# A gated mixer and state-space kernel: first layer in three tiles of 128 channels and one of 64 with stacked parts, gate sums from refetched tokens, column means on TensorE

## Chip, cores and metric

The kernel runs on one core of one Trainium2 chip. The metric is the device time of one execution in microseconds. Before the change the median of three runs is 380.77 us, from 379.42 to 381.68.

## What is computed

`x` is 2048 tokens of D = 448 channels. A sigmoid gate per token blends a state-space convolution `a` of x with a small mixer `b`:

```python
h = gelu(layernorm(x) @ w1)                      # 448 -> 448, in four groups of 112 channels
hs = concat(group 0 shifted by +1 token, group 1 by -1, group 2 by +2, group 3 by -2) @ w2
x1 = x + hs
b = x1 + gelu(layernorm(x1) @ w3) @ w4           # 448 -> 1792 -> 448
a = long_convolution(x, K) + x * D_skip
g = sigmoid((x * gate_w).sum(-1))
out = g * a + (1 - g) * b
```

The convolution's kernel K comes from 256 complex states per channel (`log_A_real`, `A_imag`, `C_real`, `C_imag`, `log_dt`). The kernel computes it by a short expansion with moments of the states, and falls back to a general path only if a guard on the data says so, which is not the case here.

## The kernel before

Tokens go in four blocks of 512, each of four chunks of 128. The matmuls are in fp32 with both factors split into a hi and a lo part, and three products are added: hi by hi, lo by hi, hi by lo.

The work is a list of 72 units. Unit n of the first 16 is a group of the shift mixer, by block in the order of groups 0, 2, 1, 3; then 56 units follow, 14 tiles of 128 channels of the second layer's 1792 for each block. Each unit has the same form:
- `first(n)`: 11 matmuls of 512 columns into a PSUM tile `p` (four k-tiles hi by hi, three lo by hi, four hi by lo). Line 437.
- `act_head(n)`: for the mixer's units a multiplication by the reciprocal deviation of each token, `rb`, on VectorE (446) and a gelu on ScalarE (456); for the others a gelu straight from PSUM (459). `act_copy(n)` rounds the result to the hi part `uh` (468), `act_tail(n)` subtracts to get the lo part `ul` on VectorE (472).
- `second(n)`: 12 matmuls of 448 columns into four PSUM tiles `acc0` to `acc3` (499), one for each chunk of the block. The last two units are in `last_two` (520).

The units 0 to 3, the loads, the splitting of W1 and W2 and the statistics of the first tokens are written out by hand in `begin()`. From unit 4 on a loop runs one iteration per unit: `first(n + 2)`, the gelu and copy of unit n + 2, the subtraction of unit n + 1, and `second(n)`. What else has to be done is put into the iterations by a table: `at(n, fn, ..., when=)` with the places before, after, between and late of iteration n. Instructions are issued on every engine in the order in which this code writes them, so the table sets what stands in front of what on each engine's queue. From iteration `OWN` on, VectorE gets the pieces of the convolution from a queue by credit.

Loads go through `room()`, which gives out three staging buffers in turn (two of the tag `raw`, one `rawc`); a load waits on SyncE (SP) until the buffer's last reader is done, and the loads behind it in SP's queue wait with it. `ld3(c)` and `ld4(i)` load pieces of W3 and W4, `sp3` and `sp4` split them: the hi part on ScalarE and the lo part on VectorE (217, 218). `ssm_par(q)` loads half of the states' parameters, `pk` (565), `ssm_exp(q)` takes their exponential (568, after a table load) and, for q = 0, a precise exponential of `log_dt` into `dts` on VectorE (65 to 79, 572, 573); `ssm_scale_par(k)` scales on ScalarE (580), and `ssm_moment(k, m)` are the moments on VectorE (586 to 599). `norm_d`, `norm_turn`, `norm_fetch`, `norm_hi` and `norm_lo` normalize a block, turn it over DRAM and split it for the second layer (382 to 406). `stats_b`, `rstd` and `rstd_rows` give means, reciprocal deviations and their rows (286 to 337); `rstd_rows` is a set of transposes on TensorE (336) and a copy on ScalarE (337).

The gate's weighted sum comes from extra columns of W1 in groups 0 and 1: `logits` copies its row out of PSUM (540) to DRAM, `logits_in` brings it back, `gates` transposes it and takes the sigmoid (554, 555), and `weigh` (410) uses it. The sums over the rows of W1 that centre it are added on GpSimd (`pool_sum`, 729 to 731) and turned into means by one matmul a group (`col_means`, 734). `keep_warm(4)` issues four matmuls into a bank that nobody reads (720).

## Time and profile before

| | before |
| --- | --- |
| median of 3 runs | 380.77 us (379.42 to 381.68) |
| the profiled execution | 380.4 us, span 378.6 us |
| granted TensorE clock | 0.997 |
| TensorE busy | 368.5 us, 97% |
| VectorE busy | 295.8 us, 78% |
| ScalarE busy | 210.2 us, 56% |
| GpSimd busy | 71.1 us, 19% |
| chain that ended last | 90% on TensorE: first layer (line 437) 46%, second layer (line 499) 43% |

The span is the time from the first to the last instruction of the profiled execution; its own time includes 1.8 us around it. Busy times are of instructions that overlap in part on TensorE, so a busy TensorE is not one at its peak. The chain of waits follows the work back from the last instruction, at each step to what released it. PE is TensorE, PEld its weight loads, DVE VectorE, ACT ScalarE, POOL GpSimd, SP and SPq SyncE and its queue of transfers. In the text iteration n is the loop's n, and unit n is finished in it by `second(n)`.

### The profile page before, as it was taken

How to read it: one execution, taken by the hardware profiler on the slowest of the kernel's cores; microseconds unless marked ns; L12 is line 12 of the kernel's file. 1: busy time of each engine (PE TensorE's matmuls, PEld its weight loads, DVE VectorE, ACT ScalarE, POOL GpSimd, SP SyncE). 2: the span in 40 equal slices, each digit the busy share in tenths (PEclk: the TensorE clock that was granted, in tenths of full speed). 3: DMA queues.
4: the chain of work that ended last, by engine and by line, in shares of the span. 5: the costliest groups of instructions: out<-in, count | busy, mean ns of one | idle time of the engine just before them, and what ended most of it. 6: DMA issues, size and time to landing. Idle time of an engine off the chain costs nothing.

```text
span 378.6 us, 5180 instructions
## 1 busy us (share of the span) xinstructions
PE 368.5 (97%) x1713; PEld 314.6 (83%) x1713; DVE 295.8 (78%) x527; ACT 210.2 (56%) x349; POOL 71.1 (19%) x187
## 2 busy tenths in 40 slices
PE   7998999999999999999999999999999999999993
PEld 4786888888888888888888888888888888888883
DVE  4888979785858981998399989999787999996312
ACT  4764646546978467643465575465756654442220
POOL 3200070322000000040023536324041440000000
PEclk9999999999999999999999999999999999999998
DMA  8970606166615219000843515256685311372202
GB/s 266 397 265 1 224 1 173 30 118 209 209 56 157 46 50 214 3 0 12 243 72 78 83 29 153 63 160 124 97 183 134 78 28 19 73 189 48 77 0 102
DMA packets 85896, 42.26 MB, mean 112 GB/s; under 512 B 67030, under 2 KB 80614, under 8 KB 85226
## 3 DMA queue, kind: packets, MB, share of 16 engines
q1 hardware_dynamic: 85434, 41.20, 41.6%
q10 hardware_dynamic: 432, 0.70, 0.6%
q8 instruction: 15, 0.25, 0.3%
q14 instruction: 15, 0.12, 0.1%
HBM read 30.86 MB, written 11.02 MB: 111 GB/s over the span
## 4 chain that ended last, share of the span: by engine, by line
PE 90%; DVE 3%; ACT 2%; DMA 2%; issue 1%; POOL 0%; SPq 0%; DVEq 0%
PE p L437 46%; PE acc L499 43%; DMA w1r<-w_in 2%; PE acc L520 1%; ACT uh L468 1%; ACT uf L456 1%; PE misc L336 0%; DVE uf L446 0%; DVE z L638 0%; DVE w2l L218 0%; DVE b L286 0%; ACT w2h L217 0%; ACT xn L294 0%; DVE ul L472 0%; DVE xh L365 0%
## 5 line engine op out<-in xcount | busy, mean ns | idle before, releaser
L459 ACT ACTIVATE uf<-p 128x512 f32<-128x512 f32 x56 | 33.4, 597 | 101.9 <-PE p L437 101.8
L472 DVE TENSOR_TENSOR ul<-uf,uh 128x512 fp32r<-128x512 f32 (+1 forms) x72 | 48.9, 680 | 31.5 <-ACT uh L468 31.4
L638 DVE TENSOR_TENSOR_SCAN z<-z,carry 128x512 f32<-128x512 f32 x48 | 61.5, 1281 | 4.6 <-ACT z L633 0.7
L437 PE MATMUL p<-xh,w3h 128*128 128x512 f32 x224 | 61.3, 396 | 0.0
L437 PE MATMUL p<-xh,w3l 128*128 128x512 f32 x224 | 60.7, 392 | 0.0
L499 PE MATMUL acc<-w4h,uh 128*128 128x448 f32 x216 | 55.8, 364 | 0.3 <-DVE xs L508 0.3
L499 PE MATMUL acc<-w4h,ul 128*128 128x448 f32 x216 | 55.7, 364 | 0.0
L499 PE MATMUL acc<-w4l,uh 128*128 128x448 f32 x216 | 55.7, 363 | 0.0
L437 PEld LDWEIGHTS p<-xh,w3l 128*128 128x128 f32 x224 | 42.1, 188 | 9.9
L437 PE MATMUL p<-xl,w3h 128*128 128x512 f32 x168 | 48.0, 394 | 0.0
L437 PEld LDWEIGHTS p<-xh,w3h 128*128 128x128 f32 x224 | 42.0, 188 | 6.7
L468 ACT ACTIVATE uh<-uf 128x512 fp32r<-128x512 f32 (+1 forms) x72 | 45.6, 633 | 2.3
L499 PEld LDWEIGHTS acc<-w4h,uh 128*128 128x128 f32 x216 | 40.5, 188 | 6.6 <-issue 0.7
L499 PEld LDWEIGHTS acc<-w4l,uh 128*128 128x128 f32 x216 | 40.5, 188 | 3.1
L499 PEld LDWEIGHTS acc<-w4h,ul 128*128 128x128 f32 x216 | 40.5, 188 | 2.9
L633 ACT ACTIVATE z<-zs,nu 128x512 f32<-128x512 f32 x64 | 42.2, 710 | 0.8 <-DMA zs<-xT_in 0.4
L632 POOL COPY z<-carry 128x1 f32<-128x1 f32 x48 | 34.6, 731 | 17.4 <-DVE zs L644 17.1
L437 PEld LDWEIGHTS p<-xl,w3h 128*128 128x128 f32 x168 | 31.5, 188 | 7.2
L323 POOL TENSOR_TENSOR t<-r 128x4 f32<-128x4 f32 (+1 forms) x15 | 6.8, 453 | 133.2 <-DVE r L321 132.5
L640 POOL COPY carry<-z 128x1 f32<-128x1 f32 x48 | 14.1, 294 | 92.4 <-DVE z L638 91.5
L456 ACT ACTIVATE uf<-uf 112x512 f32<-112x512 f32 x16 | 10.1, 630 | 24.2 <-DVE uf L446 24.1
L638 DVE TENSOR_TENSOR_SCAN z<-z,carry,zero 128x512 f32<-128x512 f32 x16 | 20.0, 1247 | 0.0
(150 smaller groups left out, 496.5 us busy)
## 6 DMA issues: line engine op xcount, KB each, us to landing
zs<-xT_in SPq DMA_DIRECT2D x4, 1024.0 KB, 8.1
yd<-yt SPq DMA_DIRECT2D x56, 64.0 KB, 2.0
ysb<-yd SPq DMA_DIRECT2D x16, 224.0 KB, 3.0
out_dram<-xs SPq DMA_DIRECT2D x16, 224.0 KB, 2.8
raw<-xb_in SPq DMA_DIRECT2D x3, 1032.0 KB, 7.9
...
```

The costliest lines, as they stand in the source:

```text
L323: eng.tensor_mul(t, y, y)
L437: nc.tensor.matmul(p[:m, t0:t1], (wl if w else wh)[:, k, :], (xl if x_ else xh)[:, k, o + t0:o + t1], start=(q == 0 and fresh), stop=stop ...
L456: nc.scalar.activation(UF[n][:m], UF[n][:m], AF.Gelu_apprx_tanh)
L459: nc.scalar.activation(UF[n][:m], P1[n][:m], AF.Gelu_apprx_tanh)
L468: nc.scalar.activation(UH[n][:m], UF[n][:m], AF.Copy)
L472: nc.vector.tensor_sub(UL[n][:m], UF.pop(n)[:m], f32(UH[n][:m]))
L499: nc.tensor.matmul(ACC[j], (UL if p == 2 else UH)[n][:m, t], wl if p == 1 else wh, start=s and p == 0, stop=e and p == 2)
L520: nc.tensor.matmul(ACC[j], (UL if p == 2 else UH)[m][:, t], wl if p == 1 else wh, start=False, stop=m > n and p == 2)
L632: nc.gpsimd.tensor_copy(z4[:, m, 0:1], carry[:, k, m:m + 1])
L633: nc.scalar.activation(z4[:, m, 1:], ZS[b][:, k, :], AF.Copy, scale=nu[:, k, m:m + 1])
L638: nc.vector.tensor_tensor_scan(z, z, up, carry[:, k, m:m + 1], OP.add, OP.add)
L640: nc.gpsimd.tensor_copy(carry[:, k, m:m + 1], z[:, TB - 1:])
```

## The change

Group 2 of the first layer keeps 64 of its 112 channels in a tile of its own. Its weights lie side by side, 64 columns of hi parts and 64 of lo parts (`w1d`), so that one pass over the hi tokens gives both products, and `first` of that unit has 7 matmuls (4 with hi tokens, 3 with lo tokens). ScalarE copies the last 64 rows out of PSUM and VectorE adds the halves (`act_add`). After the gelu the hi part goes to the first 64 rows and the lo part to the last 64 rows of one tile, against rows of W2 that are repeated, so that `second` of that unit has 8 matmuls. The other 48 channels ride, 16 each, in the tiles of groups 0, 1 and 3, which have now 128 channels. They need another token shift than the group in whose tile they are: ScalarE takes the gelu of their 16 rows from shifted columns, and a few columns from the block before, kept in `skew`. For the first block those come from a small computation of the first two tokens (`first_tokens`, `first_skew`).

The tiles have no room left for the gate's columns, so `logits`, `logits_in` and the transposing matmul go. The tokens are fetched again (`gate_fetch`), multiplied and summed on VectorE (`gate_sum`) in the iterations 18 to 25, and `gates` makes the sigmoid from an exponential in iteration 27. `weigh` moves to iteration 28 and later.

The means of W1's rows are formed by TensorE alone (`col_means`, four matmuls a group), and `pool_sum` goes. `keep_warm` isn't called any more. In the table, the statistics of blocks 0 and 1, pieces of W3 and W4, the second parameters and the moments get other iterations.

The core of the diff:

```diff
-GW = G + 2
+GX = 128 - G
+GD = G - 3 * GX
+TI = {0: 0, 1: 1, 3: 2}
+W1O = {0: 0, 2: 512, 1: 768, 3: 1280}
...
-OWN = 34
+OWN = 35
...
-    w1h, w1l = wpair([128, 4, 4, GW], "w1")
-    w2h, w2l = wpair([G, 4, D], "w2")
-    w1r = big.tile([128, 4, 4, GW], F32, name="w1r", tag="w4al")
+    w1h, w1l = wpair([128, 3, 4, 128], "w1")
+    w1d = big.tile([128, 4, 128], F32R, name="w1d", tag="w4bh")
+    w2h, w2l = wpair([128, 4, D], "w2")
+    w1r = big.tile([128, 4 * D], F32, name="w1r", tag="w4al")
+    W1R = {g: w1r[:, o:o + 4 * (GD if g == 2 else 128)].rearrange("p (k m) -> p k m", k=4) for g, o in W1O.items()}
...
-            m = GW if i < 2 else G
-            wh, wl = w1h[:, i, :, :m], w1l[:, i, :, :m]
+            wh, wl = (w1d, None) if i == 2 else (w1h[:, TI[i]], w1l[:, TI[i]])
             o = HALO - SHIFT[i]
...
-        every = [(w, x_, k, 0, TB) for w, x_, r in ((0, 0, 4), (1, 0, 4), (0, 1, 3)) for k in range(r)]
+        every = [(w, x_, k, 0, TB) for w, x_, r in ((0, 0, 4), (1, 0, 4), (0, 1, 3)) for k in range(r)
+                 if not w or wl is not None]
         for q, (w, x_, k, t0, t1) in enumerate(seq or every):
-            nc.tensor.matmul(p[:m, t0:t1], (wl if w else wh)[:, k, :], (xl if x_ else xh)[:, k, o + t0:o + t1],
+            nc.tensor.matmul(p[:, t0:t1], (wl if w else wh)[:, k, :], (xl if x_ else xh)[:, k, o + t0:o + t1],
                              start=(q == 0 and fresh), stop=stop if q + 1 == len(seq or every) else False)
...
+    def act_add(n, part=None):
+        p = P1[n]
+        if not part:
+            UF[n] = wk.tile([128, TB], F32, name="uf")
+            nc.scalar.activation(UF[n][:GD], p[GD:], AF.Copy)
+        if part is not False:
+            nc.vector.tensor_add(UF[n][:GD], p[:GD], UF[n][:GD])
+
+    MUL, EDGE = set(), {}
+
+    def act_mul_first(rows):
+
+        MUL.add(0)
+        nc.gpsimd.memset(UF[0][:, 0:1], 0.0)
+        nc.vector.tensor_mul(UF[0][:, 1:], UF[0][:, 1:], rows[:, :TB - 1])
+
     def act_mul(n):

         kind, b, i = units[n]
-        m = G if kind == "a" else 128
-        UF[n] = wk.tile([128, TB], F32, name="uf")
-        o = b * TB + HALO - SHIFT[i]
-        nc.vector.tensor_mul(UF[n][:m], P1[n][:m], rb[:m, o:o + TB])
+        p, o = P1[n], b * TB + HALO - SHIFT[i]
+        MUL.add(n)
+        if i == 2:
+            if n not in UF:
+                act_add(n)
+            nc.vector.tensor_mul(UF[n][:GD], UF[n][:GD], rb[:GD, o:o + TB])
+            return
+        if n not in UF:
+            UF[n] = wk.tile([128, TB], F32, name="uf")
+        nc.vector.tensor_mul(UF[n], p, rb[:, o:o + TB])
...
+            UL[n] = wk.tile([128, TB], F32R, name="ul", bufs=3)
+            o, sk = SHIFT[2] - SHIFT[i], skew[:, TI[i], :]
+            uf, UF[n] = UF[n], big.tile([128, TB], F32, name="ug", tag="w4bl")
+            nc.scalar.activation(UF[n], uf, AF.Gelu_apprx_tanh)
+            if n:
+                nc.scalar.activation(UF[n][:GX, :o], sk[:, SKEW - o:], AF.Gelu_apprx_tanh)
+            nc.scalar.activation(UF[n][:GX, o:], uf[:GX, :TB - o], AF.Gelu_apprx_tanh)
+            if b + 1 < NB:
+                EDGE[n] = sk, uf[:GX, TB - SKEW:]
...
-        if kind == "a" and n and (i == 0 or (i == 1 and b == NB - 1)):
-            logits(p, b, i)
...
-        nc.scalar.activation(UH[n][:m], UF[n][:m], AF.Copy)
+        kind, b, i = units[n]
+        if kind == "a" and i == 2:
+            nc.scalar.activation(UH[n][:GD], UF[n][:GD], AF.Copy)
+        else:
+            nc.scalar.activation(UH[n], UF[n], AF.Copy)
+            if n in EDGE:
+                nc.scalar.activation(*EDGE.pop(n), AF.Copy)
...
-        nc.vector.tensor_sub(UL[n][:m], UF.pop(n)[:m], f32(UH[n][:m]))
+        kind, b, i = units[n]
+        uf = UF.pop(n)
+        if kind == "a" and i == 2:
+            nc.vector.tensor_sub(UH[n][GD:], uf[:GD], f32(UH[n])[:GD])
+        else:
+            nc.vector.tensor_sub(UL[n], uf, f32(UH[n]))

     parts = {}
...
-        q = [(j, p) for p in range(3) for j in range(NT)]
+        q = [(j, p) for p in range(2 if kind == "a" and i == 2 else 3) for j in range(NT)]
...
+    GR, GT = [], {}
+
+    def gate_load():
+        GR.append(big.tile([128, D], F32, name="gr", tag="yt"))
+        nc.sync.dma_start(GR[0], gate)
+
+    def gate_fetch(j0, j1, tag):
+        t = big.tile([128, j1 - j0, D], F32, name="gx", tag=tag)
+        nc.sync.dma_start(t, x[j0 * 128:j1 * 128].rearrange("(j p) d -> p j d", p=128))
+        for j in range(j0, j1):
+            GT[j] = t[:, j - j0, :]
+
+    def gate_sum(j):
+        t = GT.pop(j)
+        nc.vector.scalar_tensor_tensor(t, t, 1.0, GR[0], op0=OP.mult, op1=OP.mult, accum_out=gg[:, j:j + 1])

     def gates():
-        p = ps.tile([128, L // 128], F32, name="misc", bufs=1)
-        nc.tensor.transpose(p, LT[0], idt[:L // 128, :L // 128])
-        nc.scalar.activation(gg, p, AF.Sigmoid)
+        nc.scalar.activation(gg, gg, AF.Exp, scale=-1.0)
+        nc.vector.tensor_scalar(gg, gg, 1.0, None, op0=OP.add)
+        nc.vector.reciprocal(gg, gg)
         nc.vector.tensor_scalar(gs, gg, -1.0, 1.0, op0=OP.mult, op1=OP.add)
...
+    def first_tokens():
+
+        e = big.tile([32, 128], F32, name="e", tag="lt")
+        p = ps.tile([2, 2 * GX], F32, name="pe", tag="acc3", bufs=1)
+        FT.extend((e, p))
+        w = w1r[:, W1O[1]:].rearrange("p (i k m) -> p i k m", i=2, k=4)
+        nc.gpsimd.memset(e, 0.0)
+        for k in range(4):
+            nc.tensor.matmul(p, xz[:, k, :], w[:, :, k, :GX], start=k == 0, stop=k == 3)
...
+        nc.vector.tensor_scalar(e[:2, :2 * GX], p, r1[:2, 0:1], None, op0=OP.mult)
+        nc.vector.transpose(e[:, 64:96], e[:, :32])
+        nc.vector.transpose(e[:, 96:128], e[:, GX:GX + 32])
+        nc.gpsimd.tensor_copy(skew[:, TI[1], 3:4], e[:GX, 64:65])
+        nc.gpsimd.tensor_copy(skew[:, TI[3], 2:4], e[:GX, 96:98])
...
-    def pool_sum(g):
-
-        if not PS:
-            PS.append(wk.tile([128, 4, G], F32, name="wsum", tag="u"))
-        t, a = PS[0][:, g], w1r[:, g, :, :G]
-        nc.gpsimd.tensor_add(t, a[:, 0, :], a[:, 1, :])
-        nc.gpsimd.tensor_add(t, t, a[:, 2, :])
-        nc.gpsimd.tensor_add(t[:64], t[:64], a[:64, 3, :])
...
     def col_means(g):
-        nc.tensor.matmul(mean_bank(g), cm[:, 0:1].to_broadcast([128, 128]), PS[0][:, g], start=True, stop=True)
+        p = mean_bank(g)
+        for k in range(4):
+            c = int(k == 3)
+            nc.tensor.matmul(p, cm[:, c:c + 1].to_broadcast([128, 128]), W1R[g][:, k, :], start=k == 0, stop=k == 3)
...
-        first(3, "misc", wh_wl[:5], stop=False)
-        rstd_rows(0, NT, "acc1")
+        first(3, "misc", wh_wl[:2], stop=False)
+        rows = rstd_rows(0, NT, "acc1")
+        act_mul_first(rows)
+        first(3, "misc", wh_wl[2:])
         rstd_rows(NT, NT + 1, "acc2")
-        act_mul(0)
-        first(3, seq=wh_wl[5:])
-        keep_warm(4)
+        first_tokens()
+        act_add(1, True)
         lo_(*s2(0))
         act_head(0)
         act_mul(1)
-        split_hi(1, 3, 4)
         act_tail(0)
+        hi(*s2(2))
         act_head(1)
         second(0)
...
+    at(4, stats_b, j2 + 1, j2 + 2)
...
+    at(6, rstd2, 0, 2)
+    at(6, stats_b, 2, 4, when=between)
...
-    for b, (n, m, q) in enumerate(((5, 6, 6), (10, 12, 12), (27, 28, 29), (34, 35, 36))):
+    for b, (n, m, q) in ((1, (16, 17, 17)), (2, (27, 28, 29)), (3, (34, 35, 36))):
...
-    at(13, logits_in)
-    at(15, gates)
-
-    for c, n, m in ((0, 5, 9), (1, 12, 14), (2, 13, 16), (3, 18, 24)):
+    at(15, gate_fetch, 0, 2, "w4bh", when=late)
+    at(15, gate_fetch, 2, 4, "w4bl", when=late)
+    at(16, gate_fetch, 4, 8, "w2h", when=late)
+    at(16, gate_fetch, 8, 12, "w2l", when=late)
+    at(19, gate_fetch, 12, 14, "w4bh", when=late)
+    at(19, gate_fetch, 14, 16, "w4bl", when=late)
+    for j, n in enumerate((18, 18, 18, 19, 20, 20, 20, 21, 21, 21, 21, 23, 25, 25, 25, 25)):
+        at(n, gate_sum, j)
+
+    for c, n, m in ((0, 5, 12), (1, 12, 14), (2, 13, 16), (3, 18, 24)):
         at(n, ld3, c)
         at(m, sp3, c, 0, when=between if c == 0 else after)
         at((12, m + 1, m + 1, m)[c], sp3, c, 2, when=between if c == 0 else after)
-    for i, n, m, a in ((0, 7, 13, (0, 4, "w4a")), (1, 15, 17, (4, 8, "w1")), (2, 19, 23, (8, 12, "w2")),
+    for i, n, m, a in ((0, 7, 14, (0, 4, "w4a")), (1, 15, 17, (4, 8, "w1")), (2, 19, 23, (8, 12, "w2")),
                        (3, 25, 26, (12, 14, "w4b"))):
         at(n, ld4, i, *a)
         for f in range(0, a[1] - a[0], 2):
-            at(m + (f // 2 if i < 2 else 0), sp4, i, f)
+            at(m + (f if i == 0 else f // 2 if i == 1 else 0), sp4, i, f)
...
+            at(max(s0 + i + 8, 28 + i // 2), weigh, b, i)
...
     at(16, ssm_par, 0)
-    at(23, ssm_par, 1)
+    at(25, ssm_par, 1, when=late)
     at(17, ssm_exp, 0)
-    at(25, ssm_exp, 1)
-    for k, q in enumerate(((18, 19, 20, 20), (21, 21, 22, 22), (25, 26, 27, 28), (29, 30, 31, 31))):
+    at(27, ssm_exp, 1)
+    at(27, gates)
+    for k, q in enumerate(((18, 19, 20, 21), (21, 22, 24, 25), (27, 28, 30, 30), (31, 31, 32, 33))):
         at(q[0] - (k == 0), ssm_scale_par, k)
...
+                if units[n + LAG][::2] == ("a", 2):
+                    act_add(n + LAG)
```

The order of instructions at the places that the prediction speaks of. First SyncE's queue in iterations 13 to 16, before: `raw` are pieces of W3 (128x4x512) and W4 (128x1792), `pk` the first parameters.

```order
42 L230 DMA raw<-w_in 128x4x512
43 L544 DMA lg<-lr 1x1
44 L550 DMA lt<-lg 16x128
45 L230 DMA raw<-w_in 128x4x512
46 L230 DMA raw<-w_in 128x1792
47 L565 DMA pk_1108<-par_in 128x2048
48 L230 DMA raw<-w_in 128x4x256
```

The same place now, with `gx` as the tokens that are fetched again:

```order
38 L236 DMA raw<-w_in 128x4x512 x2
39 L236 DMA raw<-w_in 128x1792
40 L597 DMA gx<-x_in 128x2x448 x2
41 L618 DMA pk_1115<-par_in 128x2048
42 L597 DMA gx<-x_in 128x4x448 x2
43 L236 DMA raw<-w_in 128x4x256
```

The logits' small transfers are gone, and two fetches of tokens stand between the second piece of W4 and the parameters, two more behind the parameters.

Then VectorE in iterations 14 to 17, before: `w4l_657` is the lo part of W4's first piece, whose staging buffer W4's second piece takes, the four `xs<-acc` end the last block of the shift mixer in iteration 15, and `w4l_1069` belongs to the second piece.

```order
137 L218 TENSOR_TENSOR w4l_657<-raw,w4h_656 128x896
138 L472 TENSOR_TENSOR ul<-uf,uh 112x512
139 L472 TENSOR_TENSOR ul<-uf,uh 128x512
140 L556 TENSOR_SCALAR gs<-gg 128x16
141 L218 TENSOR_TENSOR w3l<-raw,w3h 128x2x512
142 L505 TENSOR_TENSOR xs<-acc_968,xs 128x448
143 L505 TENSOR_TENSOR xs<-acc_969,xs 128x448
144 L505 TENSOR_TENSOR xs<-acc_970,xs 128x448
145 L505 TENSOR_TENSOR xs<-acc_971,xs 128x448
146 L472 TENSOR_TENSOR ul<-uf,uh 128x512
147 L218 TENSOR_TENSOR w3l<-raw,w3h 128x2x512
```

Now, where the same split is of `w4l_676`:

```order
148 L557 TENSOR_TENSOR xs<-acc_981,xs 128x448
149 L525 TENSOR_TENSOR ul<-uf,uh 128x512
150 L224 TENSOR_TENSOR w3l<-raw,w3h 128x2x512
151 L224 TENSOR_TENSOR w4l_676<-raw,w4h_675 128x896
152 L301 BN_STATS b_1129<-xs 128x6 x2
153 L303 BN_AGGR st<-b_1129 128x2 x2
154 L525 TENSOR_TENSOR ul<-uf,uh 128x512
155 L301 BN_STATS b_1160<-xs 128x6 x2
156 L303 BN_AGGR st<-b_1160 128x2 x2
```

The last split of W4's first piece stood ahead of the four additions and stands behind them now, with statistics of block 1 behind it.

Last, VectorE behind unit 19's subtraction, before and now: `rho` and `mom` are the first moments, `gx,gg` the gate's sums.

```order
167 L472 TENSOR_TENSOR ul<-uf,uh 128x512
168 L218 TENSOR_TENSOR w4l_1069<-raw,w4h_1068 128x896
169 L586 TENSOR_REDUCE rho<-pk_1108 128x2
170 L587 TENSOR_REDUCE mom<-pk_1108 128x1
171 L472 TENSOR_TENSOR ul<-uf,uh 128x512
```

```order
177 L525 TENSOR_TENSOR ul<-uf,uh 128x512
178 L603 SCALAR_TENSOR_TENSOR gx,gg<-gx,gr 128x448 x3
179 L224 TENSOR_TENSOR w4l_1070<-raw,w4h_1069 128x896
180 L639 TENSOR_REDUCE rho<-pk_1115 128x2
181 L640 TENSOR_REDUCE mom<-pk_1115 128x1
182 L525 TENSOR_TENSOR ul<-uf,uh 128x512
```

Three sums of the gate stand between the subtractions of units 19 and 20.

199 lines of the change are left out of this document (108 added, 91 removed).

## The prediction

> **What bounds the kernel now.** I read the page first, then the chain of waits, then the stretches by engine, then single engines in time.
>
> ```profile
> span 378.6 us, 5180 instructions
> PE 368.5 (97%) x1713; PEld 314.6 (83%) x1713; DVE 295.8 (78%) x527; ACT 210.2 (56%) x349; POOL 71.1 (19%) x187
> PE 90%; DVE 3%; ACT 2%; DMA 2%; issue 1%; POOL 0%; SPq 0%; DVEq 0%
> ```
>
> TensorE is busy for 97% of the span and carries 90% of the chain. So a matmul less is time less, as long as nothing else becomes late. The chain in two places, as start, length and what:
>
> ```profile
> 18.63 0.61 ACT rb L337
> 19.99 0.64 ACT uf L456
> ...
> 31.64 1.06 DVE b L286 x2
> ...
> 35.23 0.65 PE misc L336 x4
> 35.88 2.41 PE acc L499 x12
> ...
> 108.91 2.54 PE p L437 x11
> 111.45 2.42 PE acc L499 x12
> 113.87 2.54 PE p L437 x11
> 116.41 2.42 PE acc L499 x12
> ```
>
> From 18.6 to 35.2 us the chain runs through ScalarE and VectorE, so matmuls saved there (units 0 to 4) buy nothing. From 35.9 on it is eleven matmuls, twelve matmuls, and again: an iteration is 113.87 - 108.91 = 4.96 us, one first-layer matmul 2.54 / 11 = 0.231, one second-layer matmul 2.42 / 12 = 0.202. I write T17 for the start of iteration 17, 103.94 = 108.91 - 4.96 and so on; iteration 19 starts at 113.87, and its second layer needs its hi part at 116.41.
>
> **What the change removes: 4.3 us of TensorE.** A unit of 64 channels takes 7 and 8 matmuls where there were 11 and 12. Of the four, unit 1's and unit 5's first half lie in the start; what counts is units 9 and 13 in full, 2 x (4 x 0.231 + 4 x 0.202) = 3.46, and unit 5's second half, 0.81: together 4.27 us. If the start were bound by TensorE after all, another 2.65 would go; if these matmuls did not lie on the chain, nothing. The chain says they do.
>
> **The start.** Rows before the gate units:
>
> ```profile
> 19.92 1.10 PE L720 MATMUL pw<-xh,w1h 128*114 128x512 f32 x4
> 21.34 1.07 PE L499 MATMUL acc<-w2h,uh 112*128 112x448 f32 x4 [0.33 <-ACT uh L468]
> 35.23 0.65 PE L336 MATMUL misc<-idt,r 128*128 128x128 f32 x4 [1.15 <-DVE r L310]
> 18.00:38.10 20.10, 18.62 (x90) 15.31 (x89) 15.79 (x38) 11.57 (x25) 0.00 (x0) 1.00 0.39 143
> L734 PE MATMUL pm<-wsum,cm 128*128 128x112 f32 x6 | 1.3, 301 | 0.2 <-POOL wsum L731 0.2
> ```
>
> The fourth row is the stretch's time, then PE, PEld, DVE, ACT and POOL busy, the granted clock, the DMA share and GB/s. The four filler matmuls at 19.92 go, and the fifth transpose with its copy moves behind nine matmuls of unit 3 (9 x 0.231 = 2.1 us). ScalarE copies in order, so the gelu of unit 0 now comes after that copy: about 1 us later than 19.99, and second(0) about 1.3 us later than 21.34. What pays it back is unit 1's shorter first layer ahead of it (0.92) and second layer behind it (0.81). The column means on TensorE are 12 calls in place of 3; the 3 calls before were the 6 matmuls of the last row, so 18 more of some 0.1 to 0.3 us, and they stand where TensorE waited for GpSimd's sums or for W1. I take +0.3 us for the start, from -0.8 (all of it paid back and the column means free) to +1.5 (nothing paid back). TensorE will now stand still for some 1.5 us around second(0). The trace's own gap of 1.15 us left the clock at 1.00. [...]
>
> **Tokens for the gates come in by SyncE's queue.** This is the term that I trust least and that decides the sign. Rows of SP, DVE and DMA before, by start and length:
>
> ```profile
> 88.56 7.53 SPq L230 DMA_DIRECT2D raw<-w_in  x2
> 99.30 0.36 SPq L565 DMA_DIRECT2D pk<-par_in  x1
> 94.62 1.08 DVE L218 TENSOR_TENSOR w4l<-raw,w4h 128x896 fp32r<-128x896 f32 x1
> ...
> 99.19 2.21 DVE L505 TENSOR_TENSOR xs<-acc,xs 128x448 f32<-128x448 f32 x4
> 101.31 0.68 DVE L472 TENSOR_TENSOR ul<-uf,uh 128x512 fp32r<-128x512 f32 x1
> 101.91 1.22 DVE L218 TENSOR_TENSOR w3l<-raw,w3h 128x1024 fp32r<-128x1024 f32 x1
> 103.05 0.69 DVE L472 TENSOR_TENSOR ul<-uf,uh 128x512 fp32r<-128x512 f32 x1
> GB/s 0 0 0 0 0 0 0 0 243 66 88 243 397 441 441 375 419 110 0 302 126 101 227 328 353 403 454 429 378 177 0 0 0 0 0 0 0 0 66 60
> raw<-w_in SPq DMA_DIRECT2D x1, 896.0 KB, 4.5
> ```
>
> The second raw of the first row (W4's second piece, 896 KB) waits on SP until VectorE has split the last of W4's first piece: 94.62 + 1.08 = 95.70, and only then it goes. The parameters pk (1024 KB) follow at 99.30 and are in by about 103.8: the GB/s row is 94 to 107 us in 40 slices, and its data ends in the 30th. Now that split moves from iteration 14 to 16, behind the four additions, the subtraction and the split of W3 that the rows show at 99.19, 101.31 and 101.91; in the place of the row at 103.05 it would end at 103.05 + 1.08 = 104.1, which is T16 + 5.1 (T16 is 98.96). Two fetches of tokens (448 KB each) go into the queue between the raw and pk. So before pk is complete, 896 + 448 + 448 + 1024 = 2816 KB must pass. At 430 GB/s, as in the full slices, that is 6.7 us and some 2 to start and to end, as pk's own 4.5 us for 1024 KB have them; at the 300 GB/s of pk's ten slices on average it is 9.6 in all. So pk is there at T16 + 13.8 to 14.7, which is T17 + 8.8 to 9.7. Before, it was T17 - 0.1. What waits for it is ScalarE, in order:
>
> ```profile
> 105.19 1.28 ACT L568 ACT_TABLE_LOAD   x1
> 106.48 0.63 ACT L568 ACTIVATE pk<-pk 128x512 f32<-128x512 f32 x1
> 109.55 1.71 ACT L580 ACTIVATE pk<-pk,dts 128x256 f32<-128x256 f32 x4 [2.44 <-DVE dts L573]
> 111.28 1.28 ACT L459 ACT_TABLE_LOAD   x1
> 112.57 0.60 ACT L459 ACTIVATE uf<-p 128x512 f32<-128x512 f32 x1
> 113.21 0.63 ACT L468 ACTIVATE uh<-uf 128x512 fp32r<-128x512 f32 x1
> 113.87 0.69 DVE L472 TENSOR_TENSOR ul<-uf,uh 128x512 fp32r<-128x512 f32 x1 [4.34 <-ACT uh L468]
> ```
>
> From pk to the hi part of unit 19 these take 1.28 + 0.63 + 1.71 + 1.28 + 0.60 + 0.63 = 6.1 us. Before, the hi part was there at 113.84, 2.57 us ahead of 116.41, though 2.44 went into a wait for VectorE's dts; that wait now falls together with the one for pk. So the hi part comes at T17 + 14.9 to 15.8 against T17 + 12.47: TensorE stands for 2.4 to 3.3 us, and I take 2.4, since a split that is only 1 us earlier takes 1 off. Ends: 0, if the split comes much earlier; 5, if dts, which stands behind the split of the late raw on VectorE, ends after pk.
>
> [...]
>
> **Gate sums on VectorE.** Rows by form, and stretches with the columns as above:
>
> ```profile
> L668 DVE SCALAR_TENSOR_TENSOR xs<-ysb,gg,xs 128x448 f32<-128x448 f32 x16 | 10.1, 672 | 0.0
> L594 DVE DVE_READ_ACCUMULATOR mw<-mw 128x1 f32 x12 | 1.0, 82 | 0.0
> 98.80:120.00 21.20, 21.20 (x99) 18.39 (x98) 15.13 (x39) 18.48 (x28) 0.00 (x0) 1.00 0.41 135
> 120.00:140.00 20.00, 20.00 (x94) 17.38 (x94) 19.32 (x46) 11.71 (x20) 0.00 (x0) 1.00 0.25 52
> 140.00:160.00 20.00, 20.00 (x95) 17.41 (x94) 11.27 (x24) 13.28 (x21) 0.00 (x0) 1.00 0.53 123
> ```
>
> Sixteen sums of 672 + 82 ns are 12.1 us. They stand in iterations 18 to 25, 109 to 149 us, where VectorE had 19.32 of 20 busy and then 11.27 of 20. Some of the moments move later by one to two iterations to make room. Counting the instructions of each iteration by their durations before, VectorE has 4.8, 4.8, 5.2, 5.6, 4.7, 4.6, 4.3 and 4.6 us in iterations 19 to 26, 38.6 against 39.7 for TensorE. It fits by 3%, and starts late, because VectorE's subtraction of unit 19 stands behind the same late hi part (the gap of 4.34 in the last row of ScalarE's fence grows). I take 0.6 us of further waits, among them the one at units 29 and 30, where the second set of parameters needs the first set's buffer, free only after moments that now stand behind the last gate sums. From 0 to 3.
>
> **What costs nothing.**
>
> ```profile
> 38.10:58.00 19.90, 19.90 (x95) 16.77 (x95) 16.53 (x37) 11.51 (x20) 7.08 (x26) 1.00 0.33 112
> L456 ACT ACTIVATE uf<-uf 112x512 f32<-112x512 f32 x16 | 10.1, 630 | 24.2 <-DVE uf L446 24.1
> ```
>
> Each tile of 128 with foreign channels adds a gelu on 16 rows over all columns and two steps of a few columns, at most 3 x 0.63 = 1.9 us of ScalarE a unit, and I take 1; ScalarE had 11.51 busy of 19.90 there, and the rest hides it. Uncovered, the nine such units after the start would cost 9 us. The token logits went with five ScalarE copies, a transposing matmul and one table change; the gates now use the table of the parameters' second set. Statistics, transposes and turns of block 0 move in the first layer; VectorE had 16.53 of 19.90 there, with one addition more a block, so it stays short of TensorE, and I put 0.2 us for the turned block's round trip, which has 1.7 us less of matmuls to hide in.
>
> **Sum.** 380.4 is the profiled execution's own time (span 378.6 and 1.8 around it), the median of the runs 380.77. -4.27 + 0.3 + 2.4 + 0.6 + 0.2 = -0.8 us: 379.6.
>
> **Rivals.**
> A, the sum: 379.6, from 377.5 (both waits at 1 us or less, the start paid back in part) to 382. Chance 0.47.
> B, the wait at unit 19 stays hidden: VectorE does the moved split early in iteration 16, the queue runs at full rate, and what remains fits into the 2.57 us of margin and ScalarE's 2.44 of slack. For it: those two rows. Against it: one split two iterations later, in a queue that works in order. -4.27 + 0.3 + 0.2 + 0.3 = -3.5: 376.9, in the best case 375.5. Chance 0.27.
> C, slower: VectorE becomes the bound in iterations 18 to 26. It decides if its work there passes 4.96 us an iteration by some 0.3: then each of eight iterations gives it away, and the wait at unit 19 (3.3) is followed by more, since nothing behind it is idle. -4.27 + 0.3 + 3.3 + 8 x 0.4 + 0.9 = +3.4: 383.8. For it: 97% by my count, with durations from a VectorE that ran beside other loads. Against it: 11.27 busy of 20 right behind. Chance 0.21.
> D, the change leaves TensorE gaps longer than any in this trace, around second(0) and at unit 19, and the granted clock falls after them. With a first and a second layer at twice 2.54 and 2.42 us, one such place costs 5: 384.6. Against it: after 1.15 us of gap the row shows 1.00. [...] Chance 0.05.
>
> **How the numbers follow.** About 0.5%, 1.9 us, is what a measurement of this kernel can tell from no change. Faster than 378.9: all of B and 0.14 of A, 0.41. Slower than 382.7: most of C and D, 0.24. The rest, 0.35, is within. The range 375.5 to 384.0 takes in A, B and half of C; A's own is 377.5 to 382.
>
> **What would show it.** PE's busy time down by some 4 to 7 us (4 x 4 x 0.433 for the four units and 1.1 for the fillers, less the added column means). In the chain, units 9 and 13 with seven and eight matmuls. At unit 19 a gap on PE in front of acc, put down to ACT uh, and on ScalarE a wait for pk; in SP's queue the raw of W4 issued about 10 us later than 95.7, and pk behind it. If that gap is missing and the time is 377, B is right. If PE has many short gaps ahead of acc put down to DVE ul between 115 and 150, C is right. If the time is near 379.6 but the start ends 2 us later than 35.2 and no gap stands at unit 19, the sum was right by chance.

## The result, and the profile after

The kernel became slower. The median of four runs is 396.69 us (392.94 to 397.37) against 381.04 us before; the ratio is 1.0397, with a 95% interval from 1.0325 to 1.0470. The forecast was 379.6 us. The profiled execution took 397.37 us, its span is 395.6 us.

The page of the changed kernel, the lines that answer to those of before, with the granted clock in 40 slices and the chain's largest lines:

```profile
span 395.6 us, 5252 instructions
PE 372.1 (94%) x1702; PEld 317.4 (80%) x1702; DVE 307.2 (78%) x568; ACT 217.9 (55%) x385; POOL 69.4 (18%) x198
PEclk9999999999998999999999999999999987999998
PE 63%; DVE 17%; ACT 9%; DMA 4%; issue 3%; SPq 1%; POOL 1%; DVEq 0%; ACTq 0%
```

TensorE still leads, but its part of the chain fell from 90% to 63%, and VectorE and ScalarE have 26% of it. The clock line has three slices below 9, at two places, which the line of before had not; the 8 at the end stood there before. TensorE's busy time went up (372.1 us, 368.5 before) although it has fewer matmuls to do (1702, 1713 before): at half clock they took longer, as the rows of the next fence show.

The next fence is TensorE in order of time, behind the first microseconds, only its rows that began after a wait of more than half a microsecond. The bracket is the idle time ahead of the row and what ended it.

```profile
24.11 1.34 PE L551 MATMUL acc<-w2h,uh 128*128 128x448 f32 x4 [1.89 <-ACT uh L515]
36.65 0.65 PE L351 MATMUL misc<-idt,r 128*128 128x128 f32 x4 [1.32 <-DVE r L325]
42.88 0.44 PE L551 MATMUL acc<-w2h,uh 128*128 128x448 f32 x1 [0.64 <-DVE xs L557]
57.85 1.11 PE L351 MATMUL misc<-idt,r 128*128 128x128 f32 x4 [3.10 <-POOL r L341]
86.61 0.45 PE L551 MATMUL acc<-w2h,uh 128*128 128x448 f32 x1 [1.64 <-ACT uf L491]
94.95 0.96 PE L452 MATMUL p<-xh,w3h 128*128 128x512 f32 x3 [1.50 <-ACT xh L422]
125.69 1.81 PE L551 MATMUL acc<-w4h,uh 128*128 128x448 f32 x4 [2.46 <-ACT uh L515]
324.65 0.71 PE L551 MATMUL acc<-w4h,uh 128*128 128x448 f32 x1 [2.91 <-DVE xs L560]
```

The wait at 125.69 is the one that the prediction worked out for unit 19. The ones at 57.85 (iteration 7), 86.61 (iteration 12), 94.95 (iteration 14) and 324.65 (iteration 58) were not in it. The rows behind the waits at 57.85, 125.69 and 324.65 are slow: four matmuls of the second layer take 1.81 us at 125.69, at a granted clock of 0.50, where the same row takes 1.08 at full clock (the kernel with the tokens behind the parameters, below). The windows around them say why (stretch, its time, PE busy, granted clock, DMA share, GB/s):

```profile
54.10:57.51 3.41, 0.64 (x4) 1.00 0.00 0
57.51:60.92 3.41, 3.07 (x10) 0.50 0.00 0
...
122.36:125.77 3.41, 0.95 (x5) 1.00 0.72 240
125.77:129.18 3.41, 3.41 (x10) 0.50 0.00 0
...
320.33:323.75 3.42, 1.40 (x7) 1.00 0.50 77
323.75:327.16 3.41, 2.51 (x7) 0.50 0.00 0
327.16:330.57 3.41, 3.41 (x11) 0.50 0.03 5
330.57:333.98 3.41, 3.41 (x17) 1.00 0.42 78
```

After stretches of 3.41 us with 0.64, 0.95 and 1.40 us of matmuls, the next one or two of 3.41 us run at half clock. In this execution that happened after the waits in the iterations 7, 19 and 58, four such stretches in all.

How late TensorE starts an iteration, in us against the same iteration before (worked out from the starts of the first-layer groups in TensorE's rows). "Fill" is an execution without half clocks, the experiment below that fills the three long waits:

| iteration | 4 | 5 | 6 | 7 | 8 | 12 | 13 | 15 | 19 | 20 | 58 | 59 | 68 |
| --- | --- | --- | --- | --- | --- | --- | --- | --- | --- | --- | --- | --- | --- |
| changed | 1.44 | 2.31 | 1.50 | 5.20 | 5.37 | 3.69 | 5.57 | 6.99 | 6.84 | 11.14 | 11.44 | 16.21 | 16.98 |
| fill | -0.18 | 0.70 | -0.10 | 3.22 | 2.36 | 0.81 | 3.46 | 4.88 | 4.72 | 7.18 | 7.42 | 9.11 | 9.30 |

The waits of the fill row are seen as steps: 3.3 us in iteration 6 to 7, about 5 from 12 to 15 (waits in 12 and 14, less a saving), 2.5 at 19, 1.7 at 58. Between them are the small savings of the narrow units, 0.8 to 0.9 each. From 20 to 58 next to nothing changes (0.2 us), with all sixteen gate sums at its start. The 1.6 us between the rows at iteration 4 came with later first loads in that one execution; the later kernels start iteration 4 as in the fill row.

### The profile page after: what moved, and what is told of

Same layout as the page of the kernel before. It is cut to its first block, busy times and chain, and to the rows that moved or that the text cites. A ratio compares the mean times of both kernels' runs of the same rounds, so it can differ in the third digit from the quotient of the medians.

```text
span 395.6 us, 5252 instructions
## 1 busy us (share of the span) xinstructions
PE 372.1 (94%) x1702; PEld 317.4 (80%) x1702; DVE 307.2 (78%) x568; ACT 217.9 (55%) x385; POOL 69.4 (18%) x198
## 4 chain that ended last, share of the span: by engine, by line
PE 63%; DVE 17%; ACT 9%; DMA 4%; issue 3%; SPq 1%; POOL 1%; DVEq 0%; ACTq 0%
PE p L452 31%; PE acc L551 29%; DVE z L691 3%; DVE xs L557 2%; DMA pk<-par_in 2%; ACT uh L515 2%; DVE ul L525 2%; ACT ug L496 2%; DVE uf L483 2%; DVE w3l L224 1%; ACT ug L499 1%; PE acc L572 1%; DMA w1r<-w_in 1%; DVE xl L379 1%; DVE b L301 1%
## 5 line engine op out<-in xcount | busy, mean ns | idle before, releaser
L551 PE MATMUL acc<-w4h,uh 128*128 128x448 f32 x216 | 58.1, 375 | 5.4 <-DVE xs L560 2.9
L525 DVE TENSOR_TENSOR ul<-uf,uh 128x512 fp32r<-128x512 f32 x56 | 38.0, 678 | 27.3 <-ACT uh L515 27.2
L551 PE MATMUL acc<-w4l,uh 128*128 128x448 f32 x216 | 57.2, 371 | 0.0
L551 PE MATMUL acc<-w4h,ul 128*128 128x448 f32 x216 | 56.8, 369 | 0.0
L551 PEld LDWEIGHTS acc<-w4h,uh 128*128 128x128 f32 x216 | 41.4, 193 | 12.4 <-ACT z L686 3.3
L551 PEld LDWEIGHTS acc<-w4l,uh 128*128 128x128 f32 x216 | 41.6, 193 | 3.5
L515 ACT ACTIVATE uh<-uf 128x512 fp32r<-128x512 f32 x56 | 35.4, 633 | 1.8
L685 POOL COPY z<-carry 128x1 f32<-128x1 f32 x48 | 33.0, 699 | 16.0 <-DVE zs L697 15.9
L338 POOL TENSOR_TENSOR t<-r 128x4 f32<-128x4 f32 (+2 forms) x18 | 6.3, 353 | 131.7 <-DVE r L336 102.2
L551 PE MATMUL acc<-w2h,uh 128*128 128x448 f32 x64 | 19.6, 372 | 4.2 <-ACT uh L515 1.9
```

Of the source, the lines that this page charges most:

```text
L515: nc.scalar.activation(UH[n], UF[n], AF.Copy)
L525: nc.vector.tensor_sub(UL[n], uf, f32(UH[n]))
L551: nc.tensor.matmul(ACC[j], (UL if p == 2 else UH)[n][:, t], wl if p == 1 else wh, start=s and p == 0, stop=e and p == 2)
L685: nc.gpsimd.tensor_copy(z4[:, m, 0:1], carry[:, k, m:m + 1])
```

## The experiments

Theory 1 after the result: TensorE waits at five places (iterations 7, 12, 14, 19 and 58), each with a cause of its own in the order of instructions, and long waits halve the clock behind them. Theory 2: VectorE and ScalarE have no room in the first layer, so that what is taken from one wait comes back in another. The times of all kernels are device times with the kernel before run beside them (its median was 380.2 to 380.6).

**Newton steps on VectorE.**

```diff
-    at(6, rstd, r1, j2, j3, nc.gpsimd)
+    at(6, rstd, r1, j2, j3, nc.vector)
```

> One word: block 2's Newton steps for the reciprocal deviations (iteration 6) run on VectorE instead of GpSimd. In the changed kernel the transposes of iteration 7 wait 3.10 us for GpSimd's last step at 57.8 and the clock is halved right behind. Theory 1 (three waits of TensorE of 2.5 to 3.1 us, each with a cause of its own, and each followed by a window at half clock): the steps end near 55.6 instead of 57.8, the gap shrinks to under 1.2 us, no half clock at 58, TensorE 3 to 4 us earlier at iteration 8, and the time falls by 2.5 to 4 us to about 393. Theory 2 (VectorE is the bound of the first layer, so what is put on it comes back): the gap moves into iterations 8 to 14 and the time stays within 1 us.

The median is 393.99 us (392.04 to 396.64), 2.7 less than the changed kernel, with overlapping runs. TensorE's row in iteration 7:

```profile
54.68 0.62 PE L351 MATMUL misc<-idt,r 128*128 128x128 f32 x4 [1.27 <-DVE v L335]
```

The wait went from 3.10 to 1.27 us and no half clock follows it: the four first-layer matmuls behind the transposes take 1.19 us, 2.06 in the changed kernel. TensorE was 1.6 us behind at iteration 7 instead of 3.2 to 5.2, but a new wait of 1.5 us appeared in iteration 8. Both theories have a part. And a part of what is gained ahead of unit 19 comes back there: TensorE reaches iteration 17 1.9 us earlier than in the changed kernel and the parameters land only 0.9 us earlier (118.4 instead of 119.3), so its wait is 3.40 us instead of 2.46. The cause in the order: the steps stood in iteration 5 before and stand in 6 now, while the transposes that need them stayed in 7. GpSimd's last step for them, before and in the changed kernel; the transposes began at 53.21 and 57.85:

```profile
50.51 0.20 POOL L326 TENSOR_TENSOR r<-r,t 128x4 f32<-128x4 f32 x1
```

```profile
57.60 0.20 POOL L341 TENSOR_TENSOR r<-r,t 128x4 f32<-128x4 f32 x1
```

**Tokens behind the parameters.**

```diff
-    at(15, gate_fetch, 0, 2, "w4bh", when=late)
-    at(15, gate_fetch, 2, 4, "w4bl", when=late)
+    at(16, gate_fetch, 0, 2, "w4bh", when=late)
+    at(16, gate_fetch, 2, 4, "w4bl", when=late)
```

> The two token fetches that stood on SyncE's queue between W4's second piece and the parameters are issued behind the parameters (iteration 16 instead of 15). Theory 1: the parameters land about 2.1 us earlier (896 KB at 430 GB/s), the gap of 2.46 us ahead of unit 19's second layer shrinks to 0.3 or so and the half clock behind it goes (another 1.8): 4 us less, about 392.7. Theory 2 (the late split of W4's first piece alone sets it, and ScalarE or the exponential on VectorE ends later than the parameters anyway): less than 1 us.

390.62 us (389.60 to 391.93), 6 less. TensorE's wait for unit 19:

```profile
123.80 1.08 PE L551 MATMUL acc<-w4h,uh 128*128 128x448 f32 x4 [0.89 <-ACT uh L515]
```

It is 0.89 instead of 2.46 us, and four matmuls behind it take 1.08 instead of 1.81, at full clock. Theory 1 holds. The 6 us are more than the 4 that it expected: in this profile the half clock behind unit 58's wait is missing too, with a wait of 1.59 us there (the single matmuls behind it take 0.36 to 0.37 us, 0.57 in the changed kernel).

**More of the convolution ahead of block 2's end.**

```diff
-                ssm_some(n, 3.9 - (2.2
+                ssm_some(n, (4.1 if n < 55 else 3.9) - (2.2
```

> From iteration 35 to 54 VectorE is handed 4.1 us of the convolution an iteration instead of 3.9, which makes up for the queue's start one unit later (35 instead of 34). Theory 1: the gap of 2.91 us at 324 (TensorE waits for VectorE's addition of block 2 in front of unit 58) comes from the queue being one unit behind; it goes to under 1 us and with it the two windows at half clock: 4.5 to 5.3 us less, about 391.7. Theory 2 (VectorE has no room left, the added convolution comes out as a wait elsewhere): within 1 us of the changed kernel, with gaps ahead of unit 58 or between iterations 35 and 57.

394.48 us (392.45 to 398.27). The wait ahead of unit 58 stayed at 2.20 us (`DVE xs L560`), in a profile in which others had 1.6 to 2.9. So a faster queue was no cure. VectorE stands for 2.98 and 1.20 us at 292 to 297 us in this execution, waiting for the turned block 3, and has its pieces left behind that. In the changed kernel's profile these two waits were 4.08 and 1.77 us, before 1.53 and 1.47:

```profile
284.05 0.56 DVE L373 TENSOR_TENSOR xl<-xr,xh 128x384 fp32r<-128x384 f32 x1 [1.53 <-ACT xh L406]
```

```profile
297.83 0.56 DVE L389 TENSOR_TENSOR xl<-xr,xh 128x384 fp32r<-128x384 f32 x1 [4.08 <-ACT xh L422]
```

The two together are 2.85 us longer than before, and TensorE's wait ahead of unit 58 was 2.91.

**Fillers in the waits.**

```diff
+    def fill(m, kind, b):
+        p = ps.tile([128, TB], F32, name="pw", tag="misc", bufs=1)
+        w = w1h[:, 0, 0, :] if kind == "a" else w3h[:, 0, :128]
+        for _ in range(m):
+            nc.tensor.matmul(p, w, XH[kind, b][:, 0, :TB], start=True, stop=True)
...
+    at(7, fill, 10, "a", 1, when=before)
     at(7, rstd_rows, j2, j3, when=before)
+    at(19, fill, 7, "d", 0, when=late)
+    at(58, fill, 9, "d", 3, when=late)
```

> Filler matmuls into a bank that nobody reads stand in front of the three waits: 10 in iteration 7, 7 in iteration 19, 9 in iteration 58. They shorten no wait, but TensorE is busy for 2.3, 1.6 and 2.1 us of it. Theory 1 (the gaps halve the clock and that costs 1.7 + 1.7 + 3.4 us beside the waits themselves): no half clock before the end, granted clock 0.997, and 5 to 6.8 us less, about 390.5. Theory 2 (the clock falls for another reason, or the half clock costs nothing since others are waited for anyway): the time stays within 1 us, or is longer by up to 1.

389.98 us (389.75 to 390.21): 6.7 us less by 26 useless matmuls, and the runs now agree within 0.5 us, where those of the changed kernel spread over 4.4. TensorE at unit 19, and the page's clock line:

```profile
PEclk9999999999999999999999999999999999999999
...
120.95 1.79 PE L800 MATMUL pw<-xh,w3h 128*128 128x512 f32 x7
123.30 1.09 PE L551 MATMUL acc<-w4h,uh 128*128 128x448 f32 x4 [0.57 <-ACT uh L515]
```

Fillers and wait together last as long as the wait did (120.95 to 123.30, 2.35 us), so no cause of a wait was touched. What is gone is the half clock: the granted clock is 0.998 over the span, 0.978 in the changed kernel. Theory 1 holds, at the upper end of its range.

**Block-end additions ahead of the narrow unit.**

```diff
                 first(n + LAG)
+                if n in (7, 11):
+                    second(n)
                 if units[n + LAG][::2] == ("a", 2):
```

with the other call of `second` left out for these two. 

> In iterations 7 and 11 the second layer of the block's last unit and its four additions on VectorE are issued ahead of the head of the narrow unit (ScalarE's copy, VectorE's addition and multiplication), instead of behind it; TensorE's order stays. Theory 1: the gap of 1.6 to 2.4 us in front of unit 12's second layer (and of unit 8's, where it shows) is a wait for PSUM that the additions free, and these stand on VectorE behind two new operations that wait for ScalarE; with the new order it shrinks to 0.5 us or less, TensorE comes 1.5 to 2.4 us earlier to iteration 13. Theory 2 (unit 12's hi part is late itself, by the extra gelus of the foreign channels): the gap stays above 1 us. In time 1.5 to 3 us less than the changed kernel by theory 1, which the clock's windows may hide.

396.98 us (two runs). The wait in front of unit 12 fell to 0.29 us, as theory 1 said, and the one in iteration 14 rose from 1.50 to 4.36, as the second theory at the head of this section says:

```profile
83.53 0.44 PE L551 MATMUL acc<-w2h,uh 128*128 128x448 f32 x1 [0.29 <-DVE xs L557]
94.71 2.18 PE L452 MATMUL p<-xh,w3h 128*128 128x512 f32 x4 [4.36 <-ACT xh L422]
```

**W3's first half in iteration 9.**

```diff
-    for c, n, m in ((0, 5, 12), (1, 12, 14), (2, 13, 16), (3, 18, 24)):
+    for c, n, m in ((0, 5, 9), (1, 12, 14), (2, 13, 16), (3, 18, 24)):
```

> The first half of W3's first piece is split in iteration 9 again, as before the change, instead of both halves in iteration 12. Theory 1: the gap of 1.50 us in iteration 14 (first layer of unit 16 waits for ScalarE's hi part of the turned block) stands behind unit 14's multiplication on VectorE, and that behind two splits of 1.2 us; with one of them gone the gap is under 0.5 us, TensorE 1 to 1.5 us earlier at iteration 15 than 6.99 minus the other waits. Theory 2 (the turned block lands late by its round trip through DRAM): the gap stays at 1.5 and a new one of up to 1 us appears around iteration 9.

395.28 us (two runs). The wait in iteration 14 fell from 1.50 to 0.38 us; the one in front of unit 12 is 2.55.

**Less of the convolution ahead of block 2's end.**

```diff
-                ssm_some(n, 3.9 - (2.2
+                ssm_some(n, (3.1 if 54 <= n <= 57 else 3.9) - (2.2
```

> In the iterations 54 to 57 VectorE is handed 3.1 us of the convolution each instead of 3.9; what is left out comes later, where VectorE has idle time. Theory 1 (VectorE reaches the additions of block 2 late, since its queue of the convolution is one unit behind and what is in the queue in front of the additions decides): the gap in front of unit 58 (2.91 us in the profile of the changed kernel, 1.6 to 2.2 in later ones) goes to 0.3 or less, no half clock behind it; 1.7 to 5 us less. Theory 2 (the turned block 3 sets it, whose transfers come late): the gap stays at 1.5 or more.

391.53 us (two runs), 5.2 less. No wait ahead of unit 58 is left, and TensorE gains 0.5 us there where it lost 4.8. VectorE still waits 3.95 and 1.04 us for the turned block 3. Theory 1 holds in this form: with 3.2 us less work on VectorE in front of the additions, they are in time although the block is late.

**All cures so far.** The changes of the kernels on VectorE's Newton steps, tokens, additions, W3 and less convolution together, and W4's first piece in iterations 14 and 15:

```diff
-            at(m + (f if i == 0 else f // 2 if i == 1 else 0), sp4, i, f)
+            at(m + (f // 2 if i < 2 else 0), sp4, i, f)
```

> All of these together: Newton steps of block 2 on VectorE, token fetches behind the parameters, W4's first piece split in iterations 14 and 15 as before, the additions ahead of the narrow unit's head, W3's first half in iteration 9, less of the convolution in iterations 54 to 57. Theory 1 (each wait has its own cause, in the order of instructions, and what the narrow unit saves is really saved): gaps of 3.1, 2.4, 1.5, 2.5 and 1.7 us shrink to 1.5 us in sum, no half clock but perhaps one in the start, and the time is 377 to 380 us, faster than before by 0.2 to 1%. Theory 2 (VectorE and ScalarE have no room in the first layer, the waits move): 383 or more.

388.38 us (387.71 to 389.19), ratio to before 1.021 (1.0181 to 1.0239). The waits at 19 and 58 are gone. In the first layer they moved:

```profile
76.11 0.54 PE L351 MATMUL misc<-idt,r 128*128 128x128 f32 x3 [1.60 <-POOL r L341]
84.83 0.44 PE L551 MATMUL acc<-w2h,uh 128*128 128x448 f32 x1 [1.62 <-DVE xs L557]
94.88 2.18 PE L452 MATMUL p<-xh,w3h 128*128 128x512 f32 x4 [3.23 <-ACT xh L422]
```

So theory 1 is right for the places 19 and 58, and theory 2 for the first layer with these orders.

**The four cures that held**, without the additions and W3. 

> The four cures that held one by one, without the two that moved the wait elsewhere: Newton steps of block 2 on VectorE, token fetches behind the parameters, W4's first piece split in iterations 14 and 15, less of the convolution in iterations 54 to 57. Theory 1 (waits at 7, 19 and 58 have causes of their own): gaps of 1.3 us in iteration 7, none at 19 and 58; what is left is 2.4 us in iteration 12 and 1.5 in 14; TensorE is 4 us behind before from iteration 15 to the end; 383 to 386 us with the windows at half clock that are left. Theory 2 (they only hand on a lack of room in the first layer): 387 or more.

385.65 us (384.78 to 387.87), ratio 1.0167 (1.0132 to 1.0202). From iteration 20 to the end TensorE is 4.8 us behind, all of it from the first layer. Its waits there are 1.28 us in iteration 7, 1.50 in 8, 2.37 in 12 and 0.43 in 14; 1.50 were expected in 14 and none in 8. About 1.6 us of the 4.8 are a piece of half clock right behind the wait in 12, in which a second-layer matmul takes 0.57 us, 0.36 behind it.

**The same without the foreign channels' steps.** The edit leaves these out, for all units:

```diff
             nc.scalar.activation(UF[n], uf, AF.Gelu_apprx_tanh)
-            if n:
-                nc.scalar.activation(UF[n][:GX, :o], sk[:, SKEW - o:], AF.Gelu_apprx_tanh)
-            nc.scalar.activation(UF[n][:GX, o:], uf[:GX, :TB - o], AF.Gelu_apprx_tanh)
-            if b + 1 < NB:
-                EDGE[n] = sk, uf[:GX, TB - SKEW:]
```

> The kernel with the four cures, and in addition the steps for the foreign channels are left out (the two gelus on 16 rows and the copy of the last columns, so the 48 channels that ride in other tiles are not shifted in the output). Theory 1 (the first layer hangs on a chain that goes from VectorE to ScalarE and back, and 1 us more of ScalarE in each of nine units is on it): gaps of iterations 7, 12 and 14 shrink from 5.2 us to 2 or less, and TensorE is 3 to 4 us earlier at iteration 15 than with the four cures alone. Theory 2, the prediction's (ScalarE's idle time hides these steps): within 0.5 us of the four cures alone at iteration 15.

378.15 us (377.56 to 379.70), ratio to before 0.9954 (0.9939 to 0.9969), 7.5 us less than the four cures alone. ScalarE's busy time, in the page of the four cures and then of this kernel:

```profile
PE 367.6 (96%) x1702; PEld 314.0 (82%) x1702; DVE 308.0 (80%) x577; ACT 217.4 (57%) x385; POOL 69.4 (18%) x186
```

```profile
PE 364.1 (97%) x1702; PEld 311.3 (83%) x1702; DVE 307.7 (82%) x577; ACT 208.2 (55%) x353; POOL 70.4 (19%) x186
```

Of 9.2 us of ScalarE's work that is left out, 7.5 come back as time, though ScalarE is busy for a little more than half of the span. At iteration 15 TensorE is 6.6 us earlier than with the four cures alone (1.85 ahead of before, instead of 4.72 behind): more than theory 1 expected. 1.45 us of it are there at iteration 4 already. So the steps lie on the path, and theory 2 of this run, which was the prediction's, is wrong. Not all of the 7.5 us is their own length: this kernel has no half clock before its end (four second-layer matmuls take at most 1.05 us behind the start; the granted clock is 0.996 over the span), and the piece in iteration 12 of the four cures, about 1.6 us, is in the difference. The chain of waits of the four cures shows the steps in front of unit 12's second layer, whose PSUM tiles the four additions (L557) free:

```profile
79.56 0.64 ACT ug L496
80.42 0.53 ACT ug L499
80.97 0.63 ACT uh L515
81.63 0.60 ACT uf L459
82.25 0.69 DVE uf L461
82.97 0.68 DVE uf L479
83.66 2.13 DVE xs L557 x4
```

L499 is the foreign channels' gelu. The narrow unit's copy and addition (L459, L461), also new, stand in the same chain; no run leaves them out, so what they cost is not shown.

**Another order.** The four cures, with `second(n)` in iterations 7 and 11 ahead of the next unit's subtraction too, and W3's lo parts late:

```diff
-            if n < 4 * NB - 1:
+            if n < 4 * NB - 1 and n not in (7, 11):
                 act_tail(n + 1)
             if n + LAG < len(units):
                 first(n + LAG)
+                if n in (7, 11):
+                    second(n)
+                    act_tail(n + 1)
...
+        if c == 0:
+            for k in (0, 2):
+                at(m, sp3h, c, k, when=between)
+                at(m, sp3l, c, k, when=late)
+            continue
```

> The kernel with the four cures, and another order in iterations 7, 11 and 12: the block's last second layer and its four additions come ahead of the subtraction of the next unit and of the narrow unit's head, and W3's first piece gets its hi parts in the same place but its lo parts behind the multiplication of unit 14. Theory 1 (order alone makes the waits in iterations 12 and 14): the gap of 2.4 us in front of unit 12's second layer goes to 0.5 or less, the one of 1.5 in iteration 14 too; TensorE 3 us earlier at iteration 15 than with the four cures alone, and 380 to 382 us in all, no slower than before by more than 0.5%. Theory 2 (VectorE and ScalarE have too much work in a chain in the first layer): one gap goes and another grows by as much.

382.16 us (380.93 to 383.42), ratio 1.0042 (1.0023 to 1.0061). 3.5 us less than the four cures, by order alone:

```profile
81.46 0.47 PE L551 MATMUL acc<-w2h,ul 128*128 128x448 f32 x1 [0.85 <-DVE ul L525]
88.98 0.95 PE L452 MATMUL p<-xh,w3h 128*128 128x512 f32 x3 [1.07 <-ACT xh L422]
90.36 0.57 PE L452 MATMUL p<-xh,w3h 128*128 128x512 f32 x1 [0.43 <-DVE xh L390]
```

The wait in front of unit 12 is 0.85 us instead of 2.37 and the one in iteration 8 is gone, but the ones in iteration 14 are 1.5 in sum, where the four cures had 0.43: a part of the gain moved, as theory 2 said. TensorE is 2.4 us behind before from iteration 16 on. A half clock stood behind the last wait in this execution: four first-layer matmuls take 1.91 us at 90.73, 1.09 at 84.52.

**Unit 14's second layer first.**

```diff
+            if n == 14:
+                second(n)
             if n + LAG < len(units):
                 first(n + LAG)
```

> The kernel of the four cures and the new order, and TensorE takes unit 14's second layer ahead of unit 16's first layer in iteration 14, since that first layer waits there for the turned block and the second layer does not. Theory 1 (waits of TensorE in this stage are set by what stands in front of them, and where a gap falls it may halve the clock): the gaps of 1.07 and 0.43 us at 89 us go to 0.5 in sum, with them the half clock behind them in the runs that had it; 1.5 to 3 us less than 382.2, so 379 to 381, within 0.5% of the kernel before. Theory 2: unit 16's hi part becomes late instead, and the time stays at 382.

382.16 us (380.86 to 382.62), ratio 1.0040 (1.0028 to 1.0052): nothing gained. The waits at 89 are gone, and 0.94 us at 97 (for the lo part of unit 15) and 0.56 at 117 stand in their place. The time is as theory 2 said, though unit 16's hi part is not what TensorE waits for. In the profile TensorE is 1.3 us behind before at the end, with no half clock after the start (four second-layer matmuls take 1.70 us at 24.25 and at most 1.07 behind 28 us). No version that keeps the whole computation beat the kernel before.

## Why the prediction was wrong

The forecast was 17.1 us too low. The waits that its sum did not have are 9.9 us in the fill row of the table (3.3 in iteration 7, 4.9 in 12 and 14, 1.7 at 58), and the fillers took off 6.7 of half clock: 16.6 together, an estimate that adds figures of different executions.

**The saving of 4.27 us** was real. In the fill row TensorE gains 0.8 to 0.9 us at unit 5's second half, at both halves of 9 and at the first of 13; the second half of 13 stands ahead of the wait in iteration 14 and is in sight only where that is short (0.6 with the four cures).

**The start** was right in size, by luck: -0.3 to +0.1 us at iteration 4 in all eleven later profiles that keep the whole computation, 1.44 in the first. But two of its reasons were not. The gap around second(0) is 1.9 us, where some 1.5 were expected, and the sum had nothing for the clock behind it; what it cost was not measured apart. And the steps of the foreign channels are on the path there: without them iteration 4 starts 1.45 us earlier. The sum had nothing for that, and something else in the start was cheaper by as much; what, no run shows.

**The wait at unit 19** was right, and so was the chain to it. Rows of the changed kernel, SP and then ScalarE:

```profile
109.59 0.35 SPq L236 DMA_DIRECT2D raw<-w_in  x1
110.04 1.72 SPq L597 DMA_DIRECT2D gx<-x_in  x2
111.85 0.43 SPq L618 DMA_DIRECT2D pk<-par_in  x1
```

```profile
119.40 1.28 ACT L621 ACT_TABLE_LOAD   x1 [3.98 <-DMA pk<-par_in]
120.69 0.63 ACT L621 ACTIVATE pk<-pk 128x512 f32<-128x512 f32 x1
121.36 1.71 ACT L633 ACTIVATE pk<-pk,dts 128x256 f32<-128x256 f32 x4
123.08 1.28 ACT L505 ACT_TABLE_LOAD   x1
```

The raw goes at 109.59 and pk lands at 119.3, 8.7 us after iteration 17's start at 110.64; 8.8 to 9.7 were forecast. The wait is 2.46 us against 2.4; in the profiles of the other kernels with this order it is between 2.3 and 3.4. But the half clock behind it cost 1.7 more, since second(19) took 4.1 us instead of 2.4.

**What costs nothing** is the step that failed first. "ScalarE had 11.51 busy of 19.90 there, and the rest hides it": it did not. The same paragraph had the price if uncovered, 9 us; the run without these steps gained 7.5. The busy share was read as room, but the first layer goes from VectorE to ScalarE and back within each unit, both engines worked through their instructions in the order of the code (VectorE's rows at 99.19, 101.31 and 101.91 in the prediction are the instructions 142 to 147 of its order fence), and each waited for the other part of the time (the two fences below, and the L456 row). Before, the chain of waits ran on TensorE alone from 38 to 98 us, so these chains had enough lead there; how much was not worked out. The profile before held the sign already: of ScalarE's idle time there, 24.1 us were waits for VectorE's multiplication (the L456 row of the prediction). What the added link did is seen in VectorE's waits for the hi part in the first layer's units, by form before and after:

```profile
L472 DVE TENSOR_TENSOR ul<-uf,uh 112x512 fp32r<-112x512 f32 x16 | 11.0, 685 | 3.4 <-ACT uh L468 3.3
```

```profile
L525 DVE TENSOR_TENSOR ul<-ug,uh 128x512 fp32r<-128x512 f32 x12 | 8.3, 694 | 12.8 <-ACT uh L515 12.8
```

From 3.3 us in sixteen units they rose to 12.8 in twelve; with the four cures they are 11.3, and without the foreign channels' steps 5.7. Idle time that ends in a wait for the partner is no room for more links of the same chain.

**The moved statistics** are the second. The prediction took those of block 0, with 0.2 us for the turned block. But one line of the diff moves the Newton steps of block 2 from iteration 5 to 6, which put the end of GpSimd's twelve steps behind the point where TensorE reaches the transposes of iteration 7: 3.10 us, 3.3 in the table. The prediction did not name this line, nor go through who waits for each that moved; nor does the text on the change ahead of it, which speaks of blocks 0 and 1.

**VectorE ahead of block 2's end** was put at nothing. The queue of the convolution starts one unit later, which stands in the change and was not priced, and TensorE waited 1.6 to 2.9 us ahead of unit 58; the wait went with 3.2 us of work moved behind the additions. That the queue's later start is the cause is not shown: the run with more of the queue ahead gained nothing, and no run starts it in iteration 34 again. The trace of the changed kernel points at the late turned block 3, with 2.85 us more of VectorE's time spent waiting for it; why that block is late stays open.

**Rival C** (gate sums) fell: from iteration 20 to 58 TensorE loses 0.3 us against before. The sums took 9.2 us and their reads 1.3, where 12.1 were forecast.

**Rival D** was right in what the clock would do, with a chance of 0.05 that was too small: a granted clock of 0.50 after waits of 3.10, 2.46 and 2.91 us in the changed kernel, where the longest that TensorE had between its matmuls before was 1.15. The fillers took off 6.7 us. Its price was 5 us a place; four pieces of half clock cost 6.7, some 1.7 each. The profile before has half clock only at its end, behind the last matmul: 0.50 from 376.51 us on, after 3.71 us without one. The prediction weighed the gap of some 1.5 us around second(0) against the 1.15 of the trace; what the 2.4 us that its own sum has at unit 19 would do to the clock it did not ask, save in this rival.

What remains open: the first layer's waits in iterations 12 and 14 with the foreign channels' steps in place could be moved and shortened (1.3 us behind at the end in the best profile, 1.7 us in the median) but not taken away; whether a cheaper form of these steps exists was not tried.
